# Three buffers for the queries' parts, a bank apart, and square sums of heads side by side, in an attention and GEGLU block

## The chip, the cores and the metric

The kernel runs on one core of one Trainium2 chip. A core has five engines that run independently and meet through semaphores: TensorE (PE, matrix products; its weight loads are listed as PEld), VectorE (DVE), ScalarE (ACT), GpSimd (POOL) and SyncE (SP, which here only issues transfers). Data lies in SBUF (128 partitions) and in PSUM, the accumulators of TensorE: eight banks of 128 partitions by 512 f32. Transfers between memory (DRAM) and SBUF are issued by an engine's queue and carried by 16 DMA engines.

The metric is the device time of one execution in microseconds (us), as the median of several runs.

## The reference

One transformer block, all in f32: x is 2048 x 512, 32 heads of width 16 share one key and one value head, and the dense part has 1792 columns.

```python
def _A_ref(x, wq, wk, wv, wo):            # B=1, S=2048, D=512, H=32, Dh=16
    q = (x @ wq).reshape(B, S, H, Dh).transpose(0, 2, 1, 3)
    k = x @ wk                            # one key head for all
    v = x @ wv
    scores = jnp.einsum("bhqd,bkd->bhqk", q, k) * (Dh ** -0.5)
    p = softmax(scores, axis=-1)
    o = jnp.einsum("bhqk,bkd->bhqd", p, v)
    return o.transpose(0, 2, 1, 3).reshape(B, S, H * Dh) @ wo

def _B_ref(x, w_gate, w_up, w_down):      # F=1792
    return (gelu(x @ w_gate) * (x @ w_up)) @ w_down

h = x + _A_ref(_layernorm(x), wq, wk, wv, wo)
out = h + _B_ref(_layernorm(h), w_gate, w_up, w_down)
```

## The kernel before, in words

The 2048 rows are cut into four blocks b of 512 queries (T), the 512 query columns into four chunks c of 128 columns, that is eight heads each. Products that need f32 precision are made of three products of high and low parts: a value is split into a rounded high part and the rest (`split`, L123 to L128).

**The prologue** (from L1175) normalises the 16 row tiles, transposes them with TensorE, projects keys and values, and computes the first queries. TensorE also makes idle turns into a PSUM tile `idle` between the first transposes (`keep_warm`). All PSUM tiles come from `psum1` (L169): one tag "d" with 8 buffers, a bank each.

**`project_q(b, cs, eng, col)`** (L197) computes the queries of block b for the chunks cs. It is a generator: each `yield k` hands back to the schedule, which goes on with it later. For each chunk:

- 12 matmuls into a bank `pq` (L207);
- for the chunks in `HURRY` (block 0 chunk 3, block 1 chunks 0 and 1) the bank is copied out at once to `pq_raw`, by ScalarE in block 0 (L219) and VectorE in block 1 (L221);
- the high part `qh` and the low part `ql` (L226 to L228, through `split`), two buffers of each, and the squares `qs` (L231);
- three writes to `q_d` in DRAM from SP's queue (L236): for each head the rows are qh, ql, qh, then one row for a bound and one row of zeros.

After the last chunk of the call, the squares are summed over each head's 16 columns by matmuls with a 0/1 matrix `sel` into one tile `pqn` of 32 rows, one row for each head (L245, one matmul a chunk, all accumulating). VectorE copies it out (`qn`, L249) and takes its maximum over the queries into a column of `q2` (L250). POOL forms from this and from the largest key norm `k2m` two factors (`mm`, L254 to L261), and with them VectorE computes the bound row `m` from `qn` (L272), which goes to `q_d` (L274). The softmax then needs no maximum of its own.

Block 0's chunk 0 is urgent: it is computed alone, and its `m` goes from SBUF straight into the first heads' operand `qg_first` (L310). The other chunks of block 0 (`q_rest`) are begun in the prologue; the split of chunk 3 and the sums of chunks 1 to 3 come after the first scores.

**Attention, block 0** (from 47 us). For each of 8 groups of four heads and each of 16 key tiles, two score tiles of 128 keys x 2 heads x 512 queries: two matmuls (L354), one exponential on ScalarE (L358). Four value products follow, into four column groups of one bank `acc` (L362). The order is written out by hand as a string of letters, `OPENING = "ssspssps"` and then a period: s is a score tile, p goes on with the queries of later blocks (`visit`), v makes the value products of one key tile (`finish`). Now PSUM is divided anew: two score tiles of two banks ("s"), a third ("s3"), one bank for `acc`, and one bank "d", which all of `pq` and `pqn` of the later queries share, one after the other. In the first period the sums of block 0's chunks 1 to 3 follow right on block 1's chunk 0. `evacuate` (L373) copies `acc` out to `oT` and writes it to `acc_d`; the outputs come back by SP as `oc`, are divided and split into `o_hi`, `o_lo`. Meanwhile POOL splits the weights of the dense part (`part_weights`). At the end of block 0 `check_bound` (L1431) writes 32 values for a later test.

**Blocks 1 to 3 of the attention** are woven with the dense part of the block before: output projection `pp`, `pg`, `pu`, `pd` (L781), and after them the last dense block.

On TensorE, POOL, ScalarE and, from the prologue on, VectorE, instructions run in the order in which the program writes them; SP's order too is the written one from the end of the prologue on. So an instruction that waits holds up all that is behind it on its engine.

Of the kernel before, what the change touches and what calls it, by code (L numbers as in the profile page):

```python
# [28 lines left out]
FIRST_Q = 1  # L29

HURRY = ((0, 3), (1, 0), (1, 1))

OPENING = "ssspssps"

# [23 lines left out]
def kernel(  # L58
# [48 lines left out]
    nc.vector.memset(power[:, 0:1], -0.5)  # L107
    nc.vector.memset(power[:, 1:2], 0.5)

    q2 = const.tile([H, NB + 1], F32, name="q2")  # L110
    flag = const.tile([1, 1], I32, name="flag")
    kaug = const.tile([P, S], F32R, name="kaug")
    v_sb = const.tile([P, KC, 2 * DH], F32, name="v_sb")
# [44 lines left out]
    def run(outer, first):  # L158
# [8 lines left out]
        width = 0  # L167

        def psum1(name):  # L169
            if not spare:  # L170
                return ps.tile([P, T], F32, tag="d", bufs=width, name=name)
            tag, bank = take_bank(name)
            spare.append(tag)
            return bank
# [21 lines left out]

        def project_q(b, cs, eng, col):  # L197
# [4 lines left out]
            for c in cs:  # L202
                pq = psum1(f"pq_{b}_{c}")
                n = 0
                for d in range(DC):
                    for wt, xt in ((wq_hi, xT_hi), (wq_hi, xT_lo), (wq_lo, xT_hi)):
                        nc.tensor.matmul(  # L207
                            pq, wt[c][:, d, :], xt[:, d, :],
                            start=(n == 0), stop=(n == 3 * DC - 1),
                        )  # L210
                        n += 1
                    if urgent or d < DC - 1:
                        yield 3

                raw = None
                if (b, c) in HURRY:
                    raw = eb.tile([P, T], F32, tag="vT", bufs=3, name=f"pq_raw_{b}_{c}")
                    if b == 0:
                        nc.scalar.activation(raw, pq, AF.Copy)  # L219
                    else:  # L220
                        nc.vector.tensor_copy(raw, pq)  # L221
# [12 lines left out]
                qss.append(qs)  # L234
                for r0, part in ((0, qh), (DH, ql), (2 * DH, qh)):
                    nc.sync.dma_start(  # L236
                        q_d[c * HC : (c + 1) * HC, r0 : r0 + DH, tsl].bitcast(F32),
                        part.bitcast(F32),
                    )
                if raw is None or b == 0:  # L240
                    yield 4 if b > 0 and c == DC - 1 else 3

            pn = psum1(f"pqn_{b}_{cs[0]}")[:H, :]
            for i, c in enumerate(cs):
                nc.tensor.matmul(  # L245
                    pn, sel[:, c, :], qss[i], start=(i == 0), stop=(i == len(cs) - 1)
                )
            qn = eb.tile([H, T], F32, tag="qn", bufs=1, name=f"qn_{b}_{cs[0]}")
            nc.vector.tensor_copy(qn, pn)  # L249
            nc.vector.tensor_reduce(q2[:, col : col + 1], qn, axis=AX.X, op=ALU.max)  # L250
            if urgent:
                yield 2
            mm = eb.tile([H, 3], F32, tag="mm", bufs=2, name=f"mm_{b}_{cs[0]}")
            nc.gpsimd.tensor_scalar(  # L254
                mm[:, 0:1], q2[:, col : col + 1], k2m, 1e-30, op0=ALU.mult, op1=ALU.add
            )
            nc.gpsimd.tensor_tensor(mm[:, 1:2], mm[:, 0:1], power[:H, 0:1], op=ALU.pow)
# [3 lines left out]
            nc.gpsimd.tensor_scalar(  # L261
                mm[:, 1:2], mm[:, 1:2], k2m, 0.5, op0=ALU.mult, op1=ALU.mult
            )
            m = eb.tile([H, T], F32R, tag="m", bufs=2, name=f"m_{b}_{cs[0]}")
            if urgent:
                nc.scalar.activation(
                    m, qn, AF.Identity, bias=mm[:, 2:3], scale=mm[:, 1:2]
# [2 lines left out]
                return  # L270
            yield 2
            nc.vector.tensor_scalar(m, qn, mm[:, 1:2], mm[:, 2:3], op0=ALU.mult, op1=ALU.add)  # L272
            hs = slice(cs[0] * HC, (cs[-1] + 1) * HC)
            nc.sync.dma_start(q_d[hs, 3 * DH, tsl].bitcast(F32), m[hs].bitcast(F32))  # L274
            yield 0

        ms = {}
# [897 lines left out]
    def prologue(psum1, xT, wq_hi, wq_lo, sel, k2m, q_first, q_rest, advance, first_q, first_bound, eb):  # L1175
        with ExitStack() as pro:
# [25 lines left out]
            def repeat_k():  # L1202
# [16 lines left out]
            nc.gpsimd.affine_select(  # L1219
                out=sel, in_=sel, compare_op=ALU.is_ge, fill=0.0, base=DH - 1,  # L1220
                pattern=[[-P, DC], [DH, H]], channel_multiplier=-1,
            )

            bias = sb.tile([P, 1], F32, name="bias")
# [204 lines left out]
    b_d = dram.tile([1, H], F32, name="b_d")  # L1429

    def check_bound(sb, k2m):  # L1431
        q2m = sb.tile([H, 1], F32, name="q2m")
        nc.vector.tensor_reduce(q2m, q2, axis=AX.X, op=ALU.max)
        nc.vector.tensor_tensor(q2m, q2m, k2m, op=ALU.mult)
        nc.sync.dma_start(b_d.rearrange("o h -> h o"), q2m)

    def bound_flag(step):
        if step == 0:
# [74 lines left out]
```

## Time and profile before

| | us |
|---|---|
| median of 3 runs | 1410.09 (1409.43 to 1411.04) |
| the profiled execution | 1410.79 |
| its span, first to last instruction | 1409.1 |
| TensorE busy in it | 1390.7 (99%) |
| ScalarE busy | 1034.0 (73%) |
| VectorE busy | 629.8 (45%) |
| POOL busy | 231.5 (16%) |

The page shows one execution. A row of a timeline gives the start in us, the duration, the engine, the line of the program, the operation, what is written and read, and in brackets how long the engine was idle before and what ended the wait; with "x6" several instructions are merged into one row. A row of the chain that ended last gives start, length and the piece of work that the next one waited for. A row of a stretch gives its borders, its length, the busy time of PE, PEld, DVE, ACT and POOL with the number of instructions, TensorE's granted clock as a share of full speed, the DMA engines' busy share and GB/s. A row of a tile gives the shortest, median and longest duration in ns and the first and last start. Matmuls are pipelined, so the sum of their times is more than the time from one to the next, and a busy TensorE isn't TensorE at its peak.

### The profile page before, as it was taken

How to read it: one execution, taken by the hardware profiler on the slowest of the kernel's cores; microseconds unless marked ns; L12 is line 12 of the kernel's file. 1: busy time of each engine (PE TensorE's matmuls, PEld its weight loads, DVE VectorE, ACT ScalarE, POOL GpSimd, SP SyncE). 2: the span in 40 equal slices, each digit the busy share in tenths (PEclk: the TensorE clock that was granted, in tenths of full speed). 3: DMA queues.
4: the chain of work that ended last, by engine and by line, in shares of the span. 5: the costliest groups of instructions: out<-in, count | busy, mean ns of one | idle time of the engine just before them, and what ended most of it. 6: DMA issues, size and time to landing. Idle time of an engine off the chain costs nothing.

```text
span 1409.1 us, 25259 instructions
## 1 busy us (share of the span) xinstructions
PE 1390.7 (99%) x10435; PEld 760.2 (54%) x10435; DVE 629.8 (45%) x1022; ACT 1034.0 (73%) x1155; POOL 231.5 (16%) x335
## 2 busy tenths in 40 slices
PE   9999999999999999999999999999999999999998
PEld 7433333325455555555555555545555555558886
DVE  7311231214364454454354453435264453546665
ACT  7699999997877777777777777787778777762000
POOL 7575777731000000000000000000000000011000
PEclk9999999999999999999999999999999999999999
DMA  4565776745222333311432333310433332233552
GB/s 161 159 189 177 231 235 217 240 144 189 69 91 83 117 106 113 102 65 57 156 104 87 119 116 102 103 65 28 149 102 102 117 102 101 92 120 114 193 204 96
DMA packets 66707, 180.32 MB, mean 128 GB/s; under 512 B 9596, under 2 KB 9596, under 8 KB 66552
## 3 DMA queue, kind: packets, MB, share of 16 engines
q1 hardware_dynamic: 55120, 143.15, 30.7%
q0 software_dynamic: 10208, 35.26, 7.6%
q8 instruction: 84, 1.38, 0.4%
q10 hardware_dynamic: 1256, 0.20, 0.1%
q14 instruction: 39, 0.32, 0.1%
HBM read 130.87 MB, written 47.45 MB: 127 GB/s over the span
## 4 chain that ended last, share of the span: by engine, by line
PE 95%; ACT 2%; DMA 1%; DVE 1%; issue 1%; POOL 0%; SPq 0%; ACTq 0%; DVEq 0%
PE acc L362 33%; PE s L354 20%; PE pu L781 9%; PE pg L781 8%; PE pd L781 8%; PE pq L207 3%; PE pd L811 3%; PE pg L811 3%; PE pu L811 3%; PE pp L781 2%; ACT p L358 1%; PE pk L1275 1%; PE pp L883 1%; PE pd_rest L823 1%; DMA x<-in_A_x_dram 0%
## 5 line engine op out<-in xcount | busy, mean ns | idle before, releaser
L358 ACT ACTIVATE p<-s 128x1024 f32<-128x1024 f32 x1024 | 960.0, 1037 | 233.3 <-PE s L354 230.5
L362 PE MATMUL acc<-p,v_sb 128*32 128x512 f32 x4096 | 491.6, 600 | 0.0
L354 PE MATMUL s<-qg,kaug 50*128 50x512 f32 x1984 | 387.6, 426 | 4.1 <-ACT p L358 4.1
L354 PEld LDWEIGHTS s<-qg,kaug 50*128 50x128 f32 x1984 | 169.5, 184 | 282.5 <-ACT p L358 123.6
L362 PEld LDWEIGHTS acc<-p,v_sb 128*32 128x32 f32 x4096 | 108.9, 109 | 232.8 <-issue 219.9
L781 PE MATMUL pg<-x2h,w 64*128 64x512 f32 x672 | 175.2, 392 | 0.0
L781 PE MATMUL pu<-x2h,w 64*128 64x512 f32 x672 | 174.0, 392 | 0.0
L781 PE MATMUL pd<-w,gh 64*128 64x512 f32 x624 | 124.9, 393 | 1.4 <-DVE h L711 1.4
L711 DVE TENSOR_TENSOR h<-h,pd 128x512 f32<-128x512 f32 x80 | 54.4, 687 | 148.5 <-PE pd L781 148.5
L137 POOL TENSOR_SCALAR rstd<-mv 128x1 f32<-128x1 f32 x16 | 3.5, 221 | 674.0 <-DVE mv L135 673.8
L781 PEld LDWEIGHTS pg<-x2h,w 64*128 64x128 f32 x672 | 95.5, 186 | 11.3
L781 PEld LDWEIGHTS pu<-x2h,w 64*128 64x128 f32 x672 | 95.2, 186 | 11.5
L781 PE MATMUL pg<-x2l,w 64*128 64x512 f32 x336 | 100.1, 392 | 0.0
L781 PE MATMUL pu<-x2l,w 64*128 64x512 f32 x336 | 99.6, 392 | 0.0
L781 PEld LDWEIGHTS pd<-w,gh 64*128 64x128 f32 x624 | 69.6, 186 | 12.5 <-DVE h L711 2.7
L939 ACT ACTIVATE ga<-ga 128x512 f32<-128x512 f32 x14 | 8.8, 632 | 88.5 <-DVE ga L936 88.5
L781 PE MATMUL pd<-w,gl 64*128 64x512 f32 x312 | 72.7, 392 | 0.0
L375 DVE COPY oT<-acc 128x512 f32<-128x512 f32 x32 | 22.1, 690 | 112.0 <-PE acc L362 111.9
L648 DVE TENSOR_TENSOR g<-g,pg 128x512 f32<-128x512 f32 x42 | 28.8, 685 | 90.8 <-PE pg L781 90.8
L398 DVE RECIPROCAL oc<-oc 128x128 f32<-128x128 f32 x64 | 56.6, 922 | 20.2 <-DMA oc<-acc_d 16.4
L644 DVE COPY g<-pg 128x512 f32<-128x512 f32 x42 | 29.1, 692 | 72.1 <-PE pg L781 72.1
L648 DVE TENSOR_TENSOR u<-u,pu 128x512 f32<-128x512 f32 x42 | 28.8, 686 | 68.7 <-PE pu L781 68.7
(258 smaller groups left out, 1481.6 us busy)
## 6 DMA issues: line engine op xcount, KB each, us to landing
w<-w_d SPq DMA_DIRECT2D x126, 512.0 KB
w<-w_d SPq DMA_DIRECT2D x21, 1024.0 KB
qg<-q_d SPq DMA_DIRECT2D x62, 200.0 KB
q_d<-qh SPq DMA_DIRECT2D x32, 256.0 KB
acc_d<-oT SPq DMA_DIRECT2D x31, 256.0 KB
oc<-acc_d SPq DMA_DIRECT2D x124, 64.0 KB
w_d<-w_0b POOLq DMA_DIRECT2D x14, 512.0 KB, 5.0
w_d<-w_1b POOLq DMA_DIRECT2D x14, 512.0 KB, 3.3
```

The lines of the kernel that those rows point to most:

```text
L207: nc.tensor.matmul(pq, wt[c][:, d, :], xt[:, d, :], start=(n == 0), stop=(n == 3 * DC - 1),)
L354: nc.tensor.matmul(s[:, a, :], kaug[rows, kc * P : (kc + 1) * P], qg[rows, u, :], start=True, stop=True,)
L358: nc.scalar.activation(p[:, 2 * u : 2 * u + 2, :], s, AF.Exp, scale=SCALE)
L362: nc.tensor.matmul(acc[32 * j : 32 * j + 32, :], v_sb[:, kc, :], p[:, j, :], start=(kc == 0), stop=(kc == KC - 1), skip_group_check=True,)
L375: nc.vector.tensor_copy(oT, acc)
L398: nc.vector.reciprocal(oc[:, 1, sl], oc[:, 1, sl])
L644: nc.vector.tensor_copy(half, bank)
L648: nc.vector.tensor_tensor(half, half, bank, op=ALU.add)
L711: nc.vector.tensor_tensor(hs[b, t], hs[b, t], bank, op=ALU.add)
L781: nc.tensor.matmul(bank, lhsT[r], rhs[r], start=(k == 0), stop=(k == n - 1), skip_group_check=True,)
L811: nc.tensor.matmul(bank, lhsT, rhs, start=(i == 0), stop=(i == len(ts) - 1))
L823: nc.tensor.matmul(bank, lhsT, rhs, start=(i == 0), stop=(i == len(ts) - 1))
```

## The change

It has three parts, all in the making of the queries:

- `qh` and `ql` get three buffers instead of two.
- `idle`, chunk 0's and chunk 3's `pq` of block 0 share a bank of their own ("apart"); the other tiles of the prologue have seven banks instead of eight.
- `sel` is now the same small matrix for every chunk, and each chunk's sums go to 32 partitions of their own, so that the matmuls of one `pqn` write to four column groups instead of accumulating into one. The heads of chunk number i of a call stand on partitions 32 i to 32 i + 7. What follows (`qn`, `q2`, `mm`, `m`, `k2`, `k2m`, the key norms) has up to 128 partitions instead of 32; the bound rows and the bound check are written in one piece for each chunk; `m` has one buffer instead of two; and `q2` is filled with zeros at the start.

```diff
+APART = "idle", "pq_0_0", "pq_0_3"
...
-    q2 = const.tile([H, NB + 1], F32, name="q2")
+    q2 = const.tile([P, NB + 1], F32, name="q2")
...
         def psum1(name):
+            if name in APART:
+                return ps.tile([P, T], F32, tag="apart", bufs=1, name=name)
...
-            sel = eb.tile([P, DC, H], BF16, name="sel")
-            k2m = eb.tile([H, T // 32 + 1], F32, name="k2m")[:, :1]
+            sel = eb.tile([P, DC * H], BF16, name="sel")[:, :H]
+            k2m = eb.tile([P, T // 32 + 1], F32, name="k2m")[:, :1]
...
-                qh = eb.tile([P, T], F32R, tag="qh", bufs=2, name=f"qh_{b}_{c}")
-                ql = eb.tile([P, T], F32R, tag="ql", bufs=2, name=f"ql_{b}_{c}")
+                qh = eb.tile([P, T], F32R, tag="qh", bufs=3, name=f"qh_{b}_{c}")
+                ql = eb.tile([P, T], F32R, tag="ql", bufs=3, name=f"ql_{b}_{c}")
...
-            pn = psum1(f"pqn_{b}_{cs[0]}")[:H, :]
-            for i, c in enumerate(cs):
+            rows = slice(0, 32 * len(cs))
+            pn = psum1(f"pqn_{b}_{cs[0]}")[rows]
+            for i in range(len(cs)):
                 nc.tensor.matmul(
-                    pn, sel[:, c, :], qss[i], start=(i == 0), stop=(i == len(cs) - 1)
-                )
+                    pn[32 * i : 32 * i + 32, :], sel, qss[i], start=True, stop=True,
+                    skip_group_check=True,
+                )
...
-            m = eb.tile([H, T], F32R, tag="m", bufs=2, name=f"m_{b}_{cs[0]}")
+            m = eb.tile([P, T], F32R, tag="m", bufs=1, name=f"m_{b}_{cs[0]}")[rows]
...
-            hs = slice(cs[0] * HC, (cs[-1] + 1) * HC)
-            nc.sync.dma_start(q_d[hs, 3 * DH, tsl].bitcast(F32), m[hs].bitcast(F32))
+            for i, c in enumerate(cs):
+                nc.sync.dma_start(
+                    q_d[c * HC : (c + 1) * HC, 3 * DH, tsl].bitcast(F32),
+                    m[32 * i : 32 * i + HC].bitcast(F32),
+                )
...
-            width = 8
+            width = 7
...
+            nc.gpsimd.memset(q2, 0.0)
             nc.gpsimd.memset(sel, 1.0)
             nc.gpsimd.affine_select(
                 out=sel, in_=sel, compare_op=ALU.is_ge, fill=0.0, base=0,
-                pattern=[[P, DC], [-DH, H]], channel_multiplier=1,
+                pattern=[[-DH, H]], channel_multiplier=1,
             )
...
-            ones = sb.tile([DH, H], BF16, name="ones")
+            ones = sb.tile([DH, P], BF16, name="ones")
-            k2 = sb.tile([H, NB], F32, name="k2")
+            k2 = sb.tile([P, NB], F32, name="k2")
...
-                pn = psum1(f"pkn_{b}")[:H, :]
+                pn = psum1(f"pkn_{b}")
...
-        nc.sync.dma_start(b_d.rearrange("o h -> h o"), q2m)
+        for i in range(DC):
+            nc.sync.dma_start(
+                b_d[:, i * HC : (i + 1) * HC].rearrange("o h -> h o"),
+                q2m[32 * i : 32 * i + HC],
+            )
```

More of the change, by code (lines that the diff above doesn't have):

```diff
@@ L241, in project_q @@
                     yield 4 if b > 0 and c == DC - 1 else 3
-            pn = psum1(f"pqn_{b}_{cs[0]}")[:H, :]
-            for i, c in enumerate(cs):
+            rows = slice(0, 32 * len(cs))
+            pn = psum1(f"pqn_{b}_{cs[0]}")[rows]
+            for i in range(len(cs)):
                 nc.tensor.matmul(
-                    pn, sel[:, c, :], qss[i], start=(i == 0), stop=(i == len(cs) - 1)
-                )
-            qn = eb.tile([H, T], F32, tag="qn", bufs=1, name=f"qn_{b}_{cs[0]}")
+                    pn[32 * i : 32 * i + 32, :], sel, qss[i], start=True, stop=True,
+                    skip_group_check=True,
+                )
+            qn = eb.tile([P, T], F32, tag="qn", bufs=1, name=f"qn_{b}_{cs[0]}")[rows]
+            top = q2[rows, col : col + 1]
             nc.vector.tensor_copy(qn, pn)
-            nc.vector.tensor_reduce(q2[:, col : col + 1], qn, axis=AX.X, op=ALU.max)
+            nc.vector.tensor_reduce(top, qn, axis=AX.X, op=ALU.max)
             if urgent:
                 yield 2
-            mm = eb.tile([H, 3], F32, tag="mm", bufs=2, name=f"mm_{b}_{cs[0]}")
-            nc.gpsimd.tensor_scalar(
-                mm[:, 0:1], q2[:, col : col + 1], k2m, 1e-30, op0=ALU.mult, op1=ALU.add
-            )
-            nc.gpsimd.tensor_tensor(mm[:, 1:2], mm[:, 0:1], power[:H, 0:1], op=ALU.pow)
+            mm = eb.tile([P, 3], F32, tag="mm", bufs=2, name=f"mm_{b}_{cs[0]}")[rows]
+            km = k2m[rows]
+            nc.gpsimd.tensor_scalar(mm[:, 0:1], top, km, 1e-30, op0=ALU.mult, op1=ALU.add)
+            nc.gpsimd.tensor_tensor(mm[:, 1:2], mm[:, 0:1], power[rows, 0:1], op=ALU.pow)
             nc.gpsimd.tensor_scalar(
@@ L261, in project_q @@
             nc.gpsimd.tensor_scalar(
-                mm[:, 1:2], mm[:, 1:2], k2m, 0.5, op0=ALU.mult, op1=ALU.mult
+                mm[:, 1:2], mm[:, 1:2], km, 0.5, op0=ALU.mult, op1=ALU.mult
             )
-            m = eb.tile([H, T], F32R, tag="m", bufs=2, name=f"m_{b}_{cs[0]}")
+            m = eb.tile([P, T], F32R, tag="m", bufs=1, name=f"m_{b}_{cs[0]}")[rows]
             if urgent:
@@ L1220, in prologue @@
                 out=sel, in_=sel, compare_op=ALU.is_ge, fill=0.0, base=DH - 1,
-                pattern=[[-P, DC], [DH, H]], channel_multiplier=-1,
+                pattern=[[DH, H]], channel_multiplier=-1,
             )
@@ L1431, in check_bound @@
     def check_bound(sb, k2m):
-        q2m = sb.tile([H, 1], F32, name="q2m")
+        q2m = sb.tile([P, 1], F32, name="q2m")
         nc.vector.tensor_reduce(q2m, q2, axis=AX.X, op=ALU.max)
         nc.vector.tensor_tensor(q2m, q2m, k2m, op=ALU.mult)
-        nc.sync.dma_start(b_d.rearrange("o h -> h o"), q2m)
+        for i in range(DC):
[3 more added lines that the diff above has]
+            )
     def bound_flag(step):
```

## The prediction

> **What bounds the kernel now.** I read the page first, then busy time by stretches, then the ScalarE timeline and the chain that ended last, both cut to the place where ScalarE is idle.
>
> ```profile
> span 1409.1 us, 25259 instructions
> ...
> PE 95%; ACT 2%; DMA 1%; DVE 1%; issue 1%; POOL 0%; SPq 0%; ACTq 0%; DVEq 0%
> ```
>
> ```profile
> core 0: us, PE busy (x) PEld busy (x) DVE busy (x) ACT busy (x) POOL busy (x), PEclk, DMA share, GB/s
> ...
> 53.00:54.00 1.00, 0.00 (x0) 0.00 (x0) 0.97 (x3) 0.62 (x1) 0.00 (x0) 1.00 0.51 197
> 54.00:55.00 1.00, 0.00 (x0) 0.00 (x0) 1.00 (x2) 0.00 (x0) 0.00 (x0) 0.82 0.52 203
> 55.00:56.00 1.00, 0.86 (x3) 0.25 (x2) 0.09 (x1) 0.00 (x0) 0.00 (x0) 0.50 0.53 197
> ...
> 61.00:62.00 1.00, 1.00 (x8) 0.30 (x4) 0.93 (x2) 0.00 (x0) 0.63 (x2) 0.76 0.77 199
> ```
>
> ```profile
> 62.00:320.00 258.00, 255.74 (x1764) 93.09 (x1764) 57.56 (x81) 250.81 (x269) 168.21 (x204) 1.00 0.64 206
> ```
>
> TensorE carries 95% of the chain, but the change touches only the first 320 us, and there the 95% is no guide: from 62 to 320 us ScalarE's exponentials are busy 250.8 of 258 us and cannot be packed closer. Time is to be won there only where ScalarE stands idle. The ScalarE timeline has such a place just where attention begins:
>
> ```profile
> 46.62 0.60 ACT L219 ACTIVATE pq_raw<-pq 128x512 f32<-128x512 f32 x1 [1.73 <-PE pq L207]
> 47.92 5.70 ACT L358 ACTIVATE p<-s 128x1024 f32<-128x1024 f32 x6 [0.70 <-PE s L354]
> 57.35 2.85 ACT L358 ACTIVATE p<-s 128x1024 f32<-128x1024 f32 x3 [3.72 <-PE s L354]
> 62.14 13.28 ACT L358 ACTIVATE p<-s 128x1024 f32<-128x1024 f32 x14 [1.93 <-PE s L354]
> ```
>
> 0.70, 3.72 and 1.93 us are lost, 6.35 in all. The chain says why:
>
> ```profile
> 46.51 6.11 DMA q_d<-qh
> ...
> 52.73 0.44 DVE qh L127
> ...
> 55.14 1.44 PE pqn L245 x3
> ...
> 58.16 3.51 PE acc L362 x16
> 61.66 0.67 PE s L354 x4
> ```
>
> The high part of block 0's chunk 3 (L226) is third in a ring of two after chunk 1, so VectorE waits for chunk 1's last write to q_d, which lands 6.11 us after its issue. Behind it stand chunk 3's low part and squares, the copy that frees the single bank "d" (L221), the sums pqn in that bank, and, since TensorE goes in written order, all scores after the sixth. While TensorE stood still its granted clock fell from 1.00 to 0.50 and came back only near 61 us: three sums in 1.44 us, sixteen value products in 3.51. That makes the second idle time, the 1.93.
>
> **The change, part by part.**
>
> Three buffers of qh and ql.
>
> ```profile
> L236 SPq DMA_DIRECT2D q_d<-qh x32: 598/617/2020, 33.6 to 282.9; - x32
> ```
>
> Chunk 3 takes chunk 0's buffer, whose writes are the first of all, from 33.6. Then its split runs right after pq_raw (46.62 + 0.60 = 47.2) and is over before TensorE needs anything of it. What is late next is the bank "d", freed by a copy of block 1's first chunk:
>
> ```profile
> 46.14 0.39 PE L207 MATMUL pq<-xT_hi,wq_lo 128*128 128x512 f32 x1
> ...
> 47.27 1.03 PE L354 MATMUL s<-qg_first,kaug 50*128 50x512 f32 x6 [0.75 <-ACT pq_raw L219]
> ...
> 51.74 0.39 PE L207 MATMUL pq<-xT_hi,wq_lo 128*128 128x512 f32 x1
> ...
> 54.41 0.69 DVE L221 COPY pq_raw<-pq 128x512 f32<-128x512 f32 x1
> ...
> 55.14 1.44 PE L245 MATMUL pqn<-qs,sel 128*32 128x512 bf16 x3 [2.59 <-DVE pq_raw L221]
> ...
> 56.62 0.68 DVE L249 COPY qn<-pqn 32x512 f32<-32x512 f32 x1 [1.53 <-PE pqn L245]
> ```
>
> On today's clock of the timeline: the last pq product ends 51.74 + 0.39 = 52.13, the copy takes 0.69 and hands over as now in 0.04, so pqn starts at 52.9 instead of 55.14; TensorE's gap shrinks from 2.59 to about 0.4, and I expect no fall of the clock. The three sums side by side take 0.56 (worked out below): scores at 53.45, and 0.65 later (47.27 to 47.92) the seventh exponential at 54.1 instead of 57.35; ScalarE idles 0.5 (free at 47.92 + 5.70 = 53.62). Its three take 2.85, to 56.95. TensorE needs about 1.0 for six score matmuls and 1.85 for sixteen products at full clock, so the tenth score starts at 56.3 and is there at 56.95. That exponential moves from 62.14 to 56.95: gain 5.2. Bounds: if TensorE is held elsewhere until VectorE's old time, nothing; if even the 0.5 goes, 5.65.
>
> The bank apart. Today the first score waits 0.75 for ScalarE's copy of pq_0_3. In a bank of its own pq_0_3 need not share with the first scores; then TensorE could go on at once, at 46.14 + 0.32 (the step from 51.74 to the next score at 52.05) = 46.46, or when the bound's rows of m have landed. Bounds 0 (the scores still meet that bank, or wait for those rows) and 0.75; I take 0.4. The price, seven banks for the rest of the prologue, I put at nothing: chunk 0's product already holds one of the eight from the sixth row tile to the key norms, while the transposes need the most banks, and before that the warm-up turns hold it; with that cover gone it is a wait such as the 0.75.
>
> Sums side by side. Sixteen pqn matmuls stay sixteen, but those of one block go to four column groups.
>
> ```profile
> 120.83 1.85 PE acc L362 x16
> ...
> 124.15 1.03 PE L245 MATMUL pqn<-qs,sel 128*32 128x512 bf16 x4
> ...
> 125.11 0.73 PE L354 MATMUL s<-qg,kaug 50*128 50x512 f32 x4
> 125.65 1.94 ACT L358 ACTIVATE p<-s 128x1024 f32<-128x1024 f32 x2 [0.56 <-PE s L354]
> ...
> 206.95 23.62 ACT L358 ACTIVATE p<-s 128x1024 f32<-128x1024 f32 x25 [0.97 <-PE s L354]
> ...
> 286.55 5.61 ACT L358 ACTIVATE p<-s 128x1024 f32<-128x1024 f32 x6 [0.56 <-PE s L354]
> ```
>
> Four sums in a row hold up the next score by 124.15 to 125.11, 0.96 us, and ScalarE idles 0.56, 0.97 and 0.56 after each of the three. The value products already run in four groups: 1.85 for sixteen is 0.46 for a set of four. With 0.46 plus 0.1 until the next matmul, each saves 0.40, and since ScalarE's idle time is longer each time, all of it counts: 1.2. The 0.1 is my estimate, from a set that is busy 1.03 while the next matmul starts after 0.96. Bounds: 0 if they still run one after the other, 1.7 if a set costs as much as one (0.24 plus 0.1: 0.62 saved, but no more than the idle 0.56, 0.97 and 0.56 allow). [...]
>
> Everything on 128 partitions instead of 32 (qn, maxima, mm, m, key norms): nothing, because 32x512 takes 0.68 and 128x512 0.69. One buffer of m: its last readers, the writes of chunk 0's bound, are done before the next pqn. The memory fill of q2 and the smaller sel come in POOL's first stretch, and are hidden by its wait for the first statistics:
>
> ```profile
> 4.61 0.22 POOL L1245 TENSOR_SCALAR rstd<-mv 128x1 f32<-128x1 f32 x1 [0.74 <-DVE mv L1243]
> ```
>
> More writes on SP. Rows of m go out in three or four pieces, 11 issues more, and the bound check in four, 3 more. The early ones delay only q_d writes read tens of us later. The last matter, at the end of block 0:
>
> ```profile
> 126.79 0.26 POOL L254 TENSOR_SCALAR mm<-q,k2m 32x1 f32<-32x1 f32 x1 [11.62 <-ACT p L358]
> ```
>
> ```profile
> 301.36 0.53 DVE L272 TENSOR_SCALAR m<-qn,mm 32x512 fp32r<-32x512 f32 x1 [13.92 <-POOL mm L261]
> ...
> 303.04 0.69 DVE L375 COPY oT<-acc 128x512 f32<-128x512 f32 x1 [0.89 <-PE acc L362]
> ```
>
> ```profile
> 301.93 0.34 SPq L274 DMA_DIRECT2D q_d<-m  x1
> 302.36 0.37 SPq L1435 DMA_DIRECT2D b_d<-q2m  x1
> 303.76 0.34 SPq L427 DMA_DIRECT2D acc_d<-oT  x1
> ```
>
> ```profile
> 305.18 1.92 PE L362 MATMUL acc<-p,v_sb 128*32 128x512 f32 x16
> ```
>
> ```profile
> 319.04 0.69 DVE L128 TENSOR_TENSOR o_lo<-oc,o_hi 128x512 fp32r<-128x512 f32 x1
> ```
>
> ```profile
> 322.50 0.39 PE L781 MATMUL pp<-wo_hi,o_hi 64*128 64x512 f32 x1
> ```
>
> Eight issues at 0.43 (301.93 to 302.36) stand before acc_d<-oT: 301.93 + 3.44 = 305.4 instead of 303.76, 1.6 late. Besides, m hangs on POOL, which splits weights at its own pace from 128 us on. It waited 11.62 at 126.79 for q2, so it moves along with the first gains and the first saved sum (6.0), not with the last two (0.8): 2.4 late in all. The chain from acc_d ends with o_lo at 319.73, and the first dense product that reads it comes at 322.50: 2.8 to spare. So nothing, by a thin margin; bounds 0 and 1.8, if a small issue costs what those of qh do (0.617 plus the 0.09 between two, eight of them 5.7).
>
> **The sum.** 5.2 + 0.4 + 1.2 = 6.8. The profiled execution took 1410.79 (span 1409.1 and 1.7 around it), so 1404.0 on its own; it stands 0.7 above the median 1410.09, against which I forecast 1403.3, 0.48% less.
>
> **Rivals.**
> The sums gain nothing side by side: the term 1.2 is gone, and 0.2 at the start of attention; gain 5.4, 1404.7. Against it are the value products.
>
> The clock falls anyway. From pqn to the tenth score it is now 61.66 - 55.14 = 6.52 at half clock; from 52.9 that gives 59.4, and its exponential at 59.9 instead of 62.14. Gain 2.2 + 0.4 + 1.2 = 3.8, 1406.3. The trace ties the fall to the gap: 1.00 to 53.9, 0.82, 0.50. [...]
>
> The change doesn't do what it says: VectorE still waits for chunk 1's write (it needs two buffers' distance or some other thing lands then). Left are the sums: at half clock 1.44 becomes 0.92, 0.5, and 1.2 later; gain 1.7, 1408.4. Against it: the chain names that write and nothing else.
>
> The gain is given back at 300 us: POOL doesn't move (its weight loads set its pace), m stays at 301.36, the copy of acc behind it at 302.2 to 302.9, and TensorE's next value product comes at 303.0, not 305.18 - 6.8 = 298.4. It gives back 4.6: gain 2.2, 1407.9. Against it: the 11.62 that POOL waits.
>
> Slower, by SP: issues to q_d have cost SP up to 2.02 (the row of L236). With that for each of the eight, acc_d<-oT goes out at 301.93 + 16.2 = 318.1, 14.3 late, 15.1 with POOL's 0.8; less the 2.8 to spare, TensorE stands 12.3: 1410.1 - 6.8 + 12.3 = 1415.6. It decides where eight issues cost 1.8 + 2.8 - 0.8 + 6.8 = 10.6, from 1.33 each. Against it: the write of m took 0.34 and that of the bound 0.37.
>
> **Chances.** Forecast 0.60 (its own range 1402.2 to 1405.2), serial sums 0.13, clock 0.08, no effect 0.07, given back 0.07, slower 0.05. A measurement of this kernel tells about 0.2%, 2.8 us, from no change. The first three are faster, 0.81; the next two count as the same, less 0.01 to each side, 0.12; faster is then 0.82 and slower 0.06. The range runs from 1401.6 (the bounds 5.65, 0.75 and 1.7 together give 8.1, and a little) to 1407.5, which takes in the clock rival and leaves out some 2 in 10.
>
> **What would show it.** Right: no DMA in the chain near 46 to 53 us; VectorE's qh of chunk 3 at 47.3; pqn at or before 52.9 after a gap under 0.6; granted clock 1.00 throughout 50 to 62; ScalarE's idle times there 0.5 and 0; after the four sums it idles 0.40 less. First score at 46.9. Wrong: qh of chunk 3 still near 52, a clock of 0.50, a wait of pp at the first dense product, or ScalarE idle before 47 us from a wait for a bank in the prologue.

## The result, and the profile after

The changed kernel takes 1403.89 us, the median of 6 runs (1402.39 to 1405.10); the kernel before takes 1409.88 us on the same chip, also 6 runs (1409.43 to 1411.33). The ratio is 0.9957, with a 95% interval of 0.9945 to 0.9969: 6.0 us faster, between 4.4 and 7.8. The profiled execution took 1402.39 us, the least of the six. One execution of one kernel below took 1920.44 us at a mean granted clock of 0.654, and the numbers of that kernel leave it out.

The page of the changed kernel, its span and the shares of the chain that ended last:

```profile
span 1400.7 us, 25274 instructions
...
PE 95%; ACT 2%; DMA 1%; issue 1%; DVE 0%; POOL 0%; SPq 0%; ACTq 0%; DVEq 0%
```

The shares look as before. The change shows only where the prediction looked, in the first 320 us. The ScalarE timeline where attention begins (start, duration, what runs, and in brackets the idle time ahead of it with its releaser):

```profile
46.99 0.60 ACT L223 ACTIVATE pq_raw<-pq 128x512 f32<-128x512 f32 x1 [1.83 <-PE pq L211]
48.29 5.70 ACT L367 ACTIVATE p<-s 128x1024 f32<-128x1024 f32 x6 [0.70 <-PE s L363]
54.22 16.93 ACT L367 ACTIVATE p<-s 128x1024 f32<-128x1024 f32 x18 [0.23 <-PE s L363]
```

Of the idle times 0.70, 3.72 and 1.93 us of before, the 0.70 is unchanged, the second is 0.23, and the third is gone: eighteen exponentials run in one piece. The chain of the changed kernel at the same place:

```profile
52.60 0.70 DVE pq_raw L225
...
53.35 0.40 PE pqn L250 x3
53.74 0.90 PE s L363 x6
54.64 1.85 PE acc L371 x16
56.50 0.66 PE s L363 x4
```

The write to q_d is no longer in it. VectorE's and then TensorE's timeline show why:

```profile
47.62 0.82 DVE L129 CAST qh<-pq_raw 128x512 fp32r<-128x512 f32 x1 [0.59 <-ACT pq_raw L223]
...
52.60 0.69 DVE L225 COPY pq_raw<-pq 128x512 f32<-128x512 f32 x1 [0.78 <-PE pq L211]
```

```profile
47.64 1.03 PE L363 MATMUL s<-qg_first,kaug 50*128 50x512 f32 x6 [0.75 <-ACT pq_raw L223]
...
53.35 0.40 PE L250 MATMUL pqn<-qs,sel 128*32 128x512 bf16 x3 [0.42 <-DVE pq_raw L225]
```

Chunk 3's split starts as soon as ScalarE has copied the raw values out. Its three steps take 0.82, 1.65 and 1.77 us here, where the later ones of before took 0.43, 0.69 and 0.68; why is not shown. They are over at 51.82, 0.78 us ahead of the copy. The copy that frees the bank "d" waits only for the product itself, and TensorE's gap ahead of the sums is 0.42 us. The first score still waits its 0.75 for ScalarE's copy, as before. The granted clock (1.00 ahead of the DMA share and the GB/s in each row) does not fall; busy time by stretches:

```profile
54.00:55.00 1.00, 1.00 (x10) 0.37 (x10) 0.97 (x2) 0.78 (x1) 0.00 (x0) 1.00 0.52 203
55.00:56.00 1.00, 1.00 (x16) 0.26 (x8) 0.19 (x1) 1.00 (x2) 0.56 (x2) 1.00 0.53 207
```

At the three later sets of sums, TensorE's timeline for the first of them, and ScalarE's at all three:

```profile
118.97 0.40 PE L250 MATMUL pqn<-qs,sel 128*32 128x512 bf16 x4
119.29 0.73 PE L363 MATMUL s<-qg,kaug 50*128 50x512 f32 x4
```

```profile
200.55 23.63 ACT L367 ACTIVATE p<-s 128x1024 f32<-128x1024 f32 x25 [0.34 <-PE s L363]
...
285.38 15.07 ACT L367 ACTIVATE p<-s 128x1024 f32<-128x1024 f32 x16 [0.22 <-PE s L363]
```

Four sums take 0.40 us together, and the next matmul starts 0.32 after the first of them, where it was 0.96. Of ScalarE's 0.56, 0.97 and 0.56 us of idle time behind the three sets, the first and the third are gone (0.22 is its usual hand-over) and the second is 0.34.

At the end of block 0, SP's issues, then VectorE's timeline, then the first dense product:

```profile
295.27 1.31 SPq L280 DMA_DIRECT2D q_d<-m  x4
296.68 1.29 SPq L1446 DMA_DIRECT2D b_d<-q2m  x4
298.06 0.34 SPq L436 DMA_DIRECT2D acc_d<-oT  x1
```

```profile
294.70 0.55 DVE L278 TENSOR_SCALAR m<-qn,mm 128x512 fp32r<-128x512 f32 x1 [14.19 <-POOL mm L267]
...
312.46 0.69 DVE L130 TENSOR_TENSOR o_lo<-oc,o_hi 128x512 fp32r<-128x512 f32 x1
```

```profile
315.51 0.40 PE L790 MATMUL pp<-wo_hi,o_hi 64*128 64x512 f32 x1
```

The eight small writes cost SP 0.33 to 0.35 us each. The first dense product starts at 315.51 instead of 322.50: 6.99 us earlier. The rest of the program, from there to the end of the span, took 1085.2 us against 1086.6. That difference is not the change's: over thirteen profiles of eleven programs here this remainder is between 1084.8 and 1086.6, in no order that follows the edits. The start of the first dense product is therefore the steadier measure of this change, and the experiments below give it beside the times. It too moves by some 1.4 us where the clock falls on the way, as it does near 290 us in three of the profiles below.

### The profile page after: what moved, and what is told of

Same layout as the page of the kernel before. It is cut to its first block, busy times and chain, and to the rows that moved or that the text cites. A ratio compares the mean times of both kernels' runs of the same rounds, so it can differ in the third digit from the quotient of the medians.

```text
span 1400.7 us, 25274 instructions
## 1 busy us (share of the span) xinstructions
PE 1384.1 (99%) x10435; PEld 753.8 (54%) x10435; DVE 634.3 (45%) x1022; ACT 1033.6 (74%) x1155; POOL 231.6 (17%) x336
## 4 chain that ended last, share of the span: by engine, by line
PE 95%; ACT 2%; DMA 1%; issue 1%; DVE 0%; POOL 0%; SPq 0%; ACTq 0%; DVEq 0%
PE acc L371 33%; PE s L363 21%; PE pg L790 8%; PE pu L790 8%; PE pd L790 8%; PE pq L211 3%; PE pd L820 3%; PE pg L820 3%; PE pu L820 3%; PE pp L790 2%; ACT p L367 1%; PE pp L892 1%; PE pk L1285 1%; DMA x<-in_A_x_dram 1%; PE pd_rest L832 1%
```

## The experiments

The runs stood on three sets of runs of the kernel before: 1407.65 us (19 runs) for the first four kernels, 1409.04 (15 runs) for the next three and 1408.87 (10 runs) for the last four. Times are compared within a set.

**Three buffers alone.** The kernel before with

```diff
-                qh = eb.tile([P, T], F32R, tag="qh", bufs=2, name=f"qh_{b}_{c}")
-                ql = eb.tile([P, T], F32R, tag="ql", bufs=2, name=f"ql_{b}_{c}")
+                qh = eb.tile([P, T], F32R, tag="qh", bufs=3, name=f"qh_{b}_{c}")
+                ql = eb.tile([P, T], F32R, tag="ql", bufs=3, name=f"ql_{b}_{c}")
...
-            m = eb.tile([H, T], F32R, tag="m", bufs=2, name=f"m_{b}_{cs[0]}")
+            m = eb.tile([H, T], F32R, tag="m", bufs=1, name=f"m_{b}_{cs[0]}")
```

> The kernel before with three buffers of qh and ql alone (and one buffer of m, which makes the room in SBUF); sums in one column group, no bank apart. If the wait for chunk 1's write made the hole (my theory): seventh exponential near 54.4 and tenth near 57.3, first dense product near 317.2, gain 5.0, about 1404.9. If the bank apart is needed for it as well (rival): the hole stays, within 1 us of before.

Measured: 1404.30 us (8 runs, 1403.85 to 1405.81), ratio 0.9978 [0.9967, 0.9989]. Its ScalarE timeline:

```profile
48.34 5.70 ACT L358 ACTIVATE p<-s 128x1024 f32<-128x1024 f32 x6 [0.70 <-PE s L354]
54.67 16.95 ACT L358 ACTIVATE p<-s 128x1024 f32<-128x1024 f32 x18 [0.63 <-PE s L354]
```

The hole is gone with this edit alone, and with it the fall of the clock: it is at 1.00 in every stretch of 1 us from 50 to 62. From the first to the tenth exponential it is 54.67 + 3 x 0.942 - 48.34 = 9.16 us, where before had 62.14 - 47.92 = 14.22: 5.06 less in the profiles. By the times, though, the gain is 3.1 us (0.0022 of 1407.65). The step back from 5.06 to 3.1 is what the next kernels explain.

**Sums side by side alone.** The changed kernel with two buffers of qh and ql, and with all eight banks as before.

```diff
-APART = "idle", "pq_0_0", "pq_0_3"
+APART = ()
...
-                qh = eb.tile([P, T], F32R, tag="qh", bufs=3, name=f"qh_{b}_{c}")
-                ql = eb.tile([P, T], F32R, tag="ql", bufs=3, name=f"ql_{b}_{c}")
+                qh = eb.tile([P, T], F32R, tag="qh", bufs=2, name=f"qh_{b}_{c}")
+                ql = eb.tile([P, T], F32R, tag="ql", bufs=2, name=f"ql_{b}_{c}")
...
-            width = 7
+            width = 8
```

> The sums side by side alone: two buffers of qh and ql, no bank apart. Theory: the hole stays (qh of chunk 3 near 52.7, clock 0.50 after it), the sums there are 0.5 shorter, and ScalarE's idle times after the later three sums shrink by 0.6 each: first dense product near 320.2, gain 2.3, about 1407.6. Rival, that the sums alone keep TensorE warm enough: clock 1.00 and gain 4 or more.

Measured: 1405.92 us (10 runs, 1403.93 to 1407.48), ratio 0.9985 [0.9976, 0.9995], 2.1 us. VectorE, TensorE, ScalarE, and one stretch of busy time:

```profile
52.86 0.43 DVE L129 CAST qh<-pq_raw 128x512 fp32r<-128x512 f32 x1 [5.89 <-DMA q_d<-qh]
```

```profile
55.27 0.40 PE L250 MATMUL pqn<-qs,sel 128*32 128x512 bf16 x3 [2.45 <-DVE pq_raw L225]
```

```profile
56.14 16.93 ACT L367 ACTIVATE p<-s 128x1024 f32<-128x1024 f32 x18 [2.25 <-PE s L363]
```

```profile
55.00:56.00 1.00, 0.73 (x7) 0.45 (x8) 0.51 (x2) 0.00 (x0) 0.00 (x0) 1.00 0.54 209
```

The late write and TensorE's gap are there again, 5.89 and 2.45 us, but the clock stays at 1.00 here. In this execution the gap by itself does not bring the fall; the mean granted clock of the ten executions is between 0.996 and 0.999, so others may have had it. The second idle time of ScalarE is then absent, and the tenth exponential comes 10.8 us after the first (56.14 + 3 x 0.94 - 48.19) instead of 14.22.

**The bank apart taken back.** The changed kernel with the prologue's eight banks, all else as changed.

```diff
-APART = "idle", "pq_0_0", "pq_0_3"
+APART = ()
...
-            width = 7
+            width = 8
```

> The changed kernel without the bank apart: all prologue tiles from eight banks of tag d. Theory: the first score waits for ScalarE's copy of pq_0_3 with the bank apart too, so nothing is lost without it: the same time as the changed kernel to 0.3 us, about 1403.9. Rival, that the bank apart frees something in the prologue: first score later by up to 0.75, about 1404.6.

Measured: 1403.07 us (5 runs, 1401.95 to 1404.27), ratio 0.9964 [0.9951, 0.9978]. Its first scores:

```profile
47.44 1.02 PE L363 MATMUL s<-qg_first,kaug 50*128 50x512 f32 x6 [0.75 <-ACT pq_raw L223]
```

The wait is 0.75 with the bank apart and without it. This part of the change, as it stands, does nothing. (The first dense product of this profile starts at 316.63, 1.1 later than in the changed kernel, because the clock was at 0.50 from 287.7 to 291.1, where eight value products take 1.87 us instead of 1.07, and ScalarE then stood idle for 0.38 and 1.04 us.)

**The bank apart in a pool of its own.** The changed kernel gives pq_0_3 a bank apart, and yet the first score waits for ScalarE's copy of it. A possible reason is that the pool of the scores is opened only once the prologue's pool, of which the bank apart is a part, has been closed. So the edit here gives that bank a pool of its own, which is closed only after the scores' pool is open.

```diff
...
-                return ps.tile([P, T], F32, tag="apart", bufs=1, name=name)
+                return aside.tile([P, T], F32, tag="apart", bufs=1, name=name)
...
+            aside = aside_banks.enter_context(
+                tc.tile_pool(name="ps_aside", bufs=1, space=PSUM)
+            )
             set_banks("ps_pro")
...
+        aside_banks.close()
         set_banks("ps_first")
```

> The changed kernel with the bank apart in an allocation pool of its own, which is given back after the banks of the first scores. Theory: the first score waits not for a bank but for the whole pool of the prologue, so now only the third score, which takes that bank, waits for ScalarE's copy: first score 0.3 to 0.8 earlier, and all after it, about 1403.3 at best. Rival, that rows of m or something else land just then: no difference.

Measured: 1401.41 us (4 runs, 1401.07 to 1402.86), ratio 0.9950 [0.9934, 0.9967]. Its first scores:

```profile
46.65 1.32 PE L366 MATMUL s<-qg_first,kaug 50*128 50x512 f32 x6
```

The 0.75 is gone: the step from the last product of pq_0_3 to the first score is 46.65 - 46.33 = 0.32, and the exponentials begin 0.5 after ScalarE's copy begins instead of 1.3. The wait goes with the closing of the pool. That pq_0_3 and the first scores lay in different banks before this edit too is how the program allots them; no trace here shows the banks.

But the first dense product starts at 316.21, 0.7 later than in the changed kernel. ScalarE, one stretch of busy time, TensorE, and VectorE's m for block 3:

```profile
292.73 8.43 ACT L370 ACTIVATE p<-s 128x1024 f32<-128x1024 f32 x9 [1.23 <-PE s L366]
```

```profile
288.00:289.00 1.00, 1.00 (x6) 0.28 (x4) 0.00 (x0) 1.00 (x2) 0.00 (x0) 0.50 0.36 143
```

```profile
287.13 1.67 PE L374 MATMUL acc<-p,v_sb 128*32 128x512 f32 x8
```

```profile
296.27 0.55 DVE L278 TENSOR_SCALAR m<-qn,mm 128x512 fp32r<-128x512 f32 x1 [16.45 <-POOL mm L267]
```

m waits 16.45 us for GpSimd, but it runs only at 296.27, when the 1.23 us of ScalarE's idle time are over, so it can't be their cause. What stands ahead of them is a fall of the clock: the stretches of 1 us show 0.73, 0.50, 0.50 and 0.57 from 287 to 291, which is 0.50 for 3.4 us if the clock is either 1.00 or 0.50, and eight value products take 1.67 us. Sums alone (0.43 and 0.93 us of ScalarE's idle time near 292 and 295) and the bank apart taken back (0.38 and 1.04) have the same fall. A wait for GpSimd stands in two other profiles, with m at 297.58 and 297.00: there the copy of the last acc runs behind m, TensorE waits for it 0.88 us and 0.25, and ScalarE is idle for 1.15 us (two buffers of ql, below) and 0.50 (more writes on SP), against its usual 0.19.

**The clock kept up.** The kernel before, with 22 idle transposes ahead of block 0's last sums, where TensorE would stand still. They write to acc before its first real use.

```diff
+            if b == 0 and not urgent:
+                for _ in range(22):
+                    nc.tensor.transpose(acc[:, :P], ident, ident)
             pn = psum1(f"pqn_{b}_{cs[0]}")[:H, :]
```

> The kernel before with 22 idle transposes (about 2.5 us of them) on TensorE ahead of the sums of block 0's chunks 1 to 3, into the bank of acc before its first use; everything else as before, the wait for chunk 1's write too. Theory: the clock fell because of the gap, so it now stays at 1.00; pqn still starts near 55.2, the tenth score comes about 3.0 after it instead of 6.5, ScalarE's second idle time of 1.93 all but goes and its first shrinks by 0.7: gain 2.5, about 1407.4. Rival, that the clock falls anyway: no gain, or a loss of some tenths.

Measured: 1408.07 us (10 runs, 1406.37 to 1408.72), ratio 0.9996 [0.9986, 1.0006]. TensorE and ScalarE:

```profile
52.52 2.62 PE L245 MATMUL acc<-ident 128*128 128x128 f32 x22
55.11 0.81 PE L248 MATMUL pqn<-qs,sel 128*32 128x512 bf16 x3
```

```profile
47.95 5.71 ACT L361 ACTIVATE p<-s 128x1024 f32<-128x1024 f32 x6 [0.70 <-PE s L357]
56.39 16.93 ACT L361 ACTIVATE p<-s 128x1024 f32<-128x1024 f32 x18 [2.73 <-PE s L357]
```

With TensorE busy all through, the clock stays at 1.00 in every stretch of 1 us from 50 to 62: three sums take 0.81 instead of 1.44, and the 1.93 of ScalarE's idle time is gone. What is left of the hole is the wait for the write. From the first to the tenth exponential it is 56.39 + 3 x 0.94 - 47.95 = 11.26, some 3 us less than in the profile of before. The times show at most 0.0014 of 1409, 2 us, and 0.6 by the ratio. So most executions of the kernel before did not pay the whole 3 us that its profile shows. The mean granted clocks of the executions agree: of the 19 of the first set, the three with the lowest, 0.996, took 1409.02 to 1409.61 us, and the four with the highest, 0.999, took 1405.65 to 1406.16. With the transposes none of the ten is under 0.999. (The mean also counts falls in other places, so it doesn't say where they were; and the profiled execution, 1406.37, is the fastest of the ten.)

**More writes on SP.** The changed kernel with 16 writes more between block 3's m and the bound check.

```diff
+    extra_d = dram.tile([16, P // DH, T], F32, name="extra_d")
...
+            if b == NB - 1:
+                for k in range(16):
+                    nc.sync.dma_start(extra_d[k], m[0:HC].bitcast(F32))
             yield 0
```

> The changed kernel with 16 more writes of eight rows of m on SP, to a place in DRAM that nobody reads, between the last bound rows and the bound check. At 0.33 each (as in the changed kernel) acc_d<-oT goes out 5.3 later; the division's last part ended 2.4 before the first dense product needs it. Theory: that product comes 2.9 later and the time rises by 2.9, to about 1406.8. Rival, that other work covers it: no change; or that an issue costs more when many are queued: more than 5.

Measured: 1404.15 us (6 runs, 1403.40 to 1404.84), ratio 0.9966 [0.9953, 0.9978]. SP, then TensorE:

```profile
298.93 5.36 SPq L287 DMA_DIRECT2D extra_d<-m  x16
304.39 1.27 SPq L1450 DMA_DIRECT2D b_d<-q2m  x4
305.76 0.34 SPq L440 DMA_DIRECT2D acc_d<-oT  x1
```

```profile
315.80 0.39 PE L794 MATMUL pp<-wo_hi,o_hi 64*128 64x512 f32 x1
...
319.25 0.50 PE L794 MATMUL pp<-wo_hi,o_hi 64*128 64x512 f32 x2 [0.75 <-DVE o_hi L130]
```

acc_d<-oT goes out 7.7 us later than in the changed kernel (305.76 against 298.06; 2.3 of it because m comes later in this profile), and TensorE waits 0.75 us for it in all. The first dense product does not read chunk 3's values; those are the last terms of its sum. So there were 6 to 7 us to spare, and the rival, that other work covers it, held.

**Two buffers of ql.** The changed kernel with the third buffer for qh only.

```diff
-                ql = eb.tile([P, T], F32R, tag="ql", bufs=3, name=f"ql_{b}_{c}")
+                ql = eb.tile([P, T], F32R, tag="ql", bufs=2, name=f"ql_{b}_{c}")
```

> The changed kernel with two buffers of ql and three of qh. Theory: the low part of chunk 3 then waits for chunk 1's single low write, issued 0.7 before the second high write that held qh up, so VectorE goes on near 51 to 52 and frees bank d near 53.5 to 54 instead of 53.3: loss of 0 to 1 us, clock still 1.00. Rival, that both rings count the same: the hole of some 2.6 comes back.

Measured: 1404.51 us in one execution. VectorE:

```profile
51.24 0.69 DVE L130 TENSOR_TENSOR ql<-pq_raw,qh 128x512 fp32r<-128x512 f32 x1 [2.78 <-DMA q_d<-ql]
```

The low part does wait, 2.78 us for chunk 1's write, but it is over at 51.93 and the squares behind it at 52.54, just before the copy that frees the bank "d" runs, at 52.56; the seventh exponential starts at 54.18 (54.22 in the changed kernel). In this execution qh's third buffer alone brings the gain at the start.

**GpSimd out of the way, on top of the bank's own pool.** The last weight parts are issued after block 3's mm instead of ahead of it.

```diff
-                if parts is not None and n > 12 and n % 24:
-                    next(parts, None)
+                if parts is not None and n > 12 and n % 24 and n not in (232, 236):
+                    for _ in range(3 if n == 244 else 1):
+                        next(parts, None)
```

> The kernel of e4 (after, with the bank apart in a pool of its own), and GpSimd's last weight parts issued behind the four small operations of mm for the last queries. Theory (the late m of block 3's queries, 16.45 us behind GpSimd in e4 with 1.23 us of ScalarE idle at 292.7, gave part of e4's gain back): m is computed before 290, no idle time of 1 us or more on ScalarE between 285 and 300, the first dense product at 315.3 or before (e4: 316.21), and the time 0.8 to 1.2 us under e4's of the same chip. Rival (the stall is made up by the dense stage, which TensorE bounds): m is early as well, but the time stays within 0.5 us of e4's.

Measured: 1402.60 us (5 runs, 1402.31 to 1404.19), ratio 0.9958 [0.9944, 0.9971]. VectorE:

```profile
288.76 0.92 DVE L278 TENSOR_SCALAR m<-qn,mm 128x512 fp32r<-128x512 f32 x1 [9.19 <-POOL mm L267]
```

m is there 7.5 us earlier than in the first profile of the kernel with the bank's own pool, ScalarE has no idle time over 0.23 us from 285 to 313, and the first dense product starts at 314.58, the earliest of all.

**The same on the changed kernel,** without the pool of its own.

> The changed kernel with GpSimd's last weight parts behind mm, nothing else. The profile of after had m 14.19 us behind GpSimd, but hardly a stall; the profiles of e3 and e7, which start the same, had 1.0 to 1.2 us of ScalarE idle there. Theory (after loses there in some executions): 0 to 0.7 us under after's 1403.89, ratio 0.9950 to 0.9960, no idle time of ScalarE over 0.7 us between 285 and 300. Rival (no loss there): the ratio of after, 0.9957, unchanged. e8 less e9 is what the pool of its own is worth: 0.5 us by the exponentials' start.

Measured: 1403.48 us (5 runs, 1402.60 to 1404.45), ratio 0.9961 [0.9948, 0.9975]; m at 286.01, first dense product at 315.32 (315.51 in the changed kernel). No gain that the times can tell.

**The bank's own pool again,** beside these two on the same chip.

> e4 unchanged, for comparison with e8 on the same chip. Expected ratio to before 0.995, m of block 3's queries again late behind GpSimd and 0.6 to 1.4 us of ScalarE idle around 293 to 302 in its profile.

Measured: 1402.95 us (5 runs, 1401.53 to 1404.54), ratio 0.9963 [0.9950, 0.9977]. This time the clock stays at 1.00 near 290 us, and the same eight value products take 1.06 us instead of 1.67:

```profile
287.09 1.06 PE L374 MATMUL acc<-p,v_sb 128*32 128x512 f32 x8
```

m comes at 293.63, ScalarE has no idle time over 0.23 from 284 to 312, and the first dense product starts at 314.80. That is 1.41 us before that of the same program's first profile, as much as ScalarE lost there behind the fall (0.17 and 1.23). So the clock took that time back, in one execution and not in the other, and GpSimd did not. The edit that gets GpSimd out of the way is worth 0.35 us against this kernel by the medians, less than the measurement tells: the rival, at most 0.5, held. The 0.8 to 1.2 of the theory did not, since it put the 1.23 us down to m. The bank's own pool is worth 0.9 us by the medians of the two kernels that have GpSimd out of the way (1403.48 and 1402.60), and 0.74 by their first dense products; this too is under 0.2%. No kernel tried is measurably better than the changed one.

**The kernel before, once more,** unchanged, for its profile.

> The kernel before, unchanged, once more with a profile. The late q_d write again: the copy to qh of chunk 3 waits 5.5 to 6.2 us, and the gap ahead of the square sums is 2.4 to 2.7 us. If the clock falls by the length of the gap alone, it falls again after 55 (0.5 in some stretch of 1 us, second idle of ScalarE near 1.9 us, mean clock 0.996). If a gap of this length lowers it only in some executions (e2's 2.45 us did not), this profile may show 1.00 there, with a second idle of at most 0.3 us and a mean clock of 0.999.

Measured: 1408.77 us. TensorE, three stretches of busy time, and ScalarE:

```profile
55.30 1.33 PE L245 MATMUL pqn<-qs,sel 128*32 128x512 bf16 x3 [2.47 <-DVE pq_raw L221]
```

```profile
55.00:56.00 1.00, 0.70 (x3) 0.24 (x2) 0.25 (x1) 0.00 (x0) 0.00 (x0) 0.73 0.54 209
...
58.00:59.00 1.00, 1.00 (x10) 0.27 (x12) 0.06 (x1) 1.00 (x2) 0.76 (x2) 0.57 0.60 205
59.00:60.00 1.00, 1.00 (x16) 0.17 (x8) 0.22 (x1) 1.00 (x2) 0.56 (x3) 1.00 0.66 168
```

```profile
57.40 2.86 ACT L358 ACTIVATE p<-s 128x1024 f32<-128x1024 f32 x3 [3.50 <-PE s L354]
60.87 14.21 ACT L358 ACTIVATE p<-s 128x1024 f32<-128x1024 f32 x15 [0.61 <-PE s L354]
```

The clock falls again, but for a shorter time. If it is either 1.00 or 0.50, the 0.73 puts the fall at 55.46 and the 0.57 its end at 58.86: 3.4 us. In the first profile the same reckoning (0.82 from 54 to 55, 0.76 from 61 to 62) gives 54.64 to 61.48: 6.8 us, twice that. The tenth exponential comes 60.87 - 48.20 = 12.67 us after the first, between 14.22 and the 10.8 of the kernel in which the clock did not fall.

The landmarks together (first dense product, and what remains of the span from there):

| kernel | ratio to before | first dense product, us | rest, us |
|---|---|---|---|
| before | 1 | 322.50 | 1086.6 |
| before, once more | 1 | 321.23 | 1085.8 |
| clock kept up | 0.9996 | 319.46 | 1085.1 |
| sums side by side alone | 0.9985 | 318.73 | 1086.6 |
| three buffers alone | 0.9978 | 317.76 | 1086.3 |
| bank apart taken back | 0.9964 | 316.63 | 1084.8 |
| two buffers of ql (one execution) | - | 316.39 | 1086.4 |
| more writes on SP | 0.9966 | 315.80 | 1086.1 |
| changed kernel | 0.9957 | 315.51 | 1085.2 |
| own pool (two profiles) | 0.9950, 0.9963 | 316.21, 314.80 | 1084.9, 1085.0 |
| changed, GpSimd out of the way | 0.9961 | 315.32 | 1086.5 |
| own pool, GpSimd out of the way | 0.9958 | 314.58 | 1086.0 |

Three of these starts have the fall near 290 us in them: sums alone, the bank apart taken back, and the first of the two profiles with the own pool. ScalarE's idle time behind it is 1.36, 1.42 and 1.40 us.

## Why the prediction was right, and where it was not

The forecast was 1403.3 us, 0.48% less; measured were 1403.89 and 0.43%. By the profiles, the sum of 6.8 us stands against 6.99 at the first dense product. Two terms were off, in opposite directions, and a third is right only for executions like the one it was read from.

**Three buffers, 5.2.** Every step of it happened: qh of chunk 3 at 47.62 (47.3 was said, and this execution was 0.37 late from its first loads on), a gap of 0.42 (0.4), no fall of the clock, no second idle time. From the first to the tenth exponential the changed kernel takes 54.22 + 3 x 0.941 - 48.29 = 8.75 us, 5.47 less than before. That ScalarE idles 0.23 there and not 0.5 comes from the sums, 0.32 to the next matmul instead of 0.56. The undoing of one part shows it as cause: with two buffers the 5.89 and the 2.45 are back, with three alone they are gone.

The step that was mis-sized is "I expect no fall of the clock", or rather its other half: that the kernel before always has one. Against the two profiles of before, three buffers alone gain 5.06 and 12.67 - 9.16 = 3.5 us at the tenth exponential; its measured gain is 3.1. The term was right for the execution that had been profiled, one with a long fall, and too large for the median.

**"The trace ties the fall to the gap".** One trace did, with a gap of 2.59 us. The clock fell behind 2.47 in another execution too, but stayed at 1.00 behind 2.45 in a third. By the stretches of 1 us it was at 0.50 for 6.8 us and for 3.4. Nor does the length of the gap settle it later: the three falls near 290 us came behind gaps of 0.71 and 0.41 us, 1.1 in all, and the other ten profiles have the same two gaps there, to 0.01 us, without a fall (the mean clock from 62 to 320 us is 0.99 in the three and 1.00 in the ten). What decides is not shown here. A gap of 2.59 should have been put as enough in some executions.

**The bank apart, 0.4.** Wrong; it is its lower bound, 0. The step that failed is "In a bank of its own pq_0_3 need not share with the first scores; then TensorE could go on at once". With a bank of its own in the prologue's pool the wait stays at 0.75; it goes with that pool. With a pool of its own the scores start 0.32 after the last product, as the prediction had reckoned: the step was right about TensorE and wrong about what the wait hangs on. Its price, seven banks, was nothing, as said: with eight the first score starts at 47.44, with seven at 47.64, and the kernel before has 47.27 and 47.55 in its two profiles.

**Sums side by side, 1.2.** The mechanism held, and the term was too small: 0.56 + 0.63 + 0.56 = 1.75 of ScalarE's idle time is gone, its upper bound. A set of four does not run in the 0.46 + 0.1 of the f32 value products but in 0.40, with the next matmul after 0.32. The upper bound, a set that costs as much as one with 0.34 to the next matmul, was the nearer one here: 0.96 to 0.32 is three times. Alone, the part gains 2.1 us, the 1.75 and what it saves at the start.

**SP, nothing.** Right, with a wider margin than given. An issue cost 0.33 to 0.35 us, not 0.43, and the 2.8 to spare was taken to the wrong reader: the first dense product reads the other chunks first. Sixteen writes more cost TensorE 0.75 us.

**GpSimd moves along.** m came at 294.70 instead of 301.36, 6.7 earlier where 6.0 was said, in the profile that was taken. Two other profiles of almost the same program show the rival in a small form: m at 297.00 and 297.58, and 0.50 and 1.15 us of ScalarE's idle time behind it, not 4.6. In the medians it is not seen.

The other rivals: the clock did not fall near 55 us in the profile of the changed kernel, the sums were not serial, the buffers did what the change says, and SP did not make it slower.

Taken together, the two parts that do something gain 3.1 and 2.1 us alone, and 5.1 together without the bank apart (0.0036 of 1407.65). The 6.0 of the changed kernel on its chip has an interval of 4.4 to 7.8, so no further cause is needed. The forecast came near because the 0.4 that wasn't there and the surplus in the buffers' term were about made up by the sums. That was luck.

## What to carry to other kernels

When one profile shows a lowered clock behind a short gap, take a second profile before pricing it: the fall here cost nothing, 1.4 or 3.0 us in executions with about the same gap (the tenth exponential came 12.67 and 14.22 us after the first, against 11.26 with the clock kept up), beside the 2.1 that the late write cost in all of them (11.26 against 9.16). Before a stall is put down to an instruction that ran late near it, see that the instruction ran ahead of the stall, and look at the clock: 1.23 us of idle time that seemed to come from a late m had ended 3.5 us before m ran, and stood behind a fall of the clock. Giving a tile its own bank frees nothing if the wait hangs on the pool that it is allocated from (0.75 us here with the bank apart and without it, none with a pool of its own); look for the wait in the timeline after the edit. And to find how much room a late transfer has, find the first instruction that reads it, not the first of the group that it belongs to.

## What the runs showed of the hardware

- The granted clock went from 1.00 to 0.50 for 3.4 us and for 6.8 us, worked out from the stretches of 1 us, behind gaps of TensorE of 2.47 and 2.59 us, and not at all behind one of 2.45. In three of thirteen profiles it fell behind gaps of 0.71 and 0.41 us, which the other ten have too, to 0.50 for 3.4 us by the stretches of two of the three; behind it ScalarE was idle for 1.36 to 1.42 us.
- Four bf16 matmuls of 128x512 to four column groups take 0.40 us together, where one alone takes 0.39, and the next matmul starts 0.32 us after the first.
- The rest of this program from the first dense product on took 1084.8 to 1086.6 us in the profiles, a spread of 1.8 us with no edit behind it; below that, a landmark inside the program tells more than the whole time.
